# The first 512 tokens of a gated SSM and feed-forward mix: token tiles turned by the matrix engine instead of a transposing DMA, and weight strips taken in order of landing

## The chip, the cores and the metric

The kernel runs on one core of one Trainium2 chip, in one launch. The metric is the device time of the execution in microseconds (us); the time before is the median of nine runs. One execution was also profiled.

Names used below: PE is the matrix engine (TensorE), PEld its weight loads, DVE the vector engine, ACT the scalar engine, POOL GpSimd, SP the sync engine. SP and ACT issue DMAs; their issues are shown as SPq and ACTq.

## The reference

The input `x` has 2048 tokens of 640 channels, in bf16. Three things are computed from it and mixed:

```
g = sigmoid((x * gate_w).sum(-1, keepdims=True))        # one gate for each token
# branch A: diagonal complex state-space layer, P = 640 states
Lam_bar = exp(exp(log_dt) * Lam)
B_bar   = ((Lam_bar - 1) / Lam)[:, None] * (B_re + 1j*B_im)
h_t     = Lam_bar * h_{t-1} + B_bar x_t
a       = 2 * real(h @ C.T) + x * Dskip
# branch B: feed-forward, 640 -> 1728 -> 640
b       = gelu_tanh(x @ w1 + b1) @ w2 + b2
out     = g * a + (1 - g) * b
```

## The kernel before, in words

Tokens are worked in `NCH` = 4 chunks of `CH` = 512, each of four token tiles of `P` = 128. The 640 channels are `KD` = 5 blocks of 128 (`kd` = 0 to 4). A matmul needs the channels on the partitions, so each chunk needs `x` turned: `xT[c]`, of shape 128 x 5 x 512. For chunks 1 to 3 a transposing DMA on SP makes it. For chunk 0 there are two ways side by side. Token tiles 0 and 1 are loaded as they lie (`xn[0]`), and `turn` makes a matmul of the tile against an identity, five per token tile, into a PSUM bank; `turned` copies the bank into `xT[0]`, on DVE or on ACT. Token tiles 2 and 3 (tokens `HT` = 256 to 511) are written by one transposing DMA on SP (line 141).

The first feed-forward matmul (FF1) of chunk 0 fills `FA` = 6 PSUM banks at once, one for each 128-wide block `kf` of the 1728 hidden units. It goes by strips: `strip(kd, t0, t1, first)` issues six matmuls, one for each bank, with the weights `w1a[kd]` (128 x 768) and the tokens `t0` to `t1` (line 247 in `ff1_mm`). So PE can begin a strip as soon as that `w1a[kd]` and that token tile are there. The order before is: kd 0 for tile 0; tile 1 is turned; kd 1 for tile 0; kd 0 and 1 for tile 1; kd 2 for tiles 0 and 1; a small matmul that turns the parameter rows `prmA` (line 322); kd 3 and 4 for tiles 0 and 1; then kd 0 to 4 for tiles 2 and 3 (256 columns each), with a small matmul on `prmB` (line 379) after kd 2. Six gelus on ACT (line 252, with the bias `colB` that comes from `prmB`) empty the six banks. The next hidden blocks use `w1b` and go bank by bank: the first two fill two banks that are free, and the third needs one of the six.

Beside this runs a chain for the rotation tables of the state-space scan: `prmA` is copied to `colA` on DVE (line 323), then one small `Exp` on ACT, small products on DVE, three wide DVE instructions (lines 354 to 356, `u`, `kk`, `red`), the `Sin` activations on ACT (lines 365 to 374), and from line 394 on the DVE work that builds the tables `TCOS` and `TSIN`. The scan of all chunks follows on DVE.

What sets the order. On PE, DVE and ACT the instructions run in the order in which the kernel writes them (`manual_schedule`); an engine's next instruction waits behind the one before it. DMAs run in the order of issue on their queue. The program hands out eight completion semaphores to the DMAs in turn, over both queues, and an issue waits until the earlier DMA with the same semaphore has landed: so the second `w1a` on ACT, `w1a[2]`, is issued when `w1a[0]` has landed, and what is behind it on that queue waits too. The initial issues before are: on SP `xn` tile 0, `xn` tile 1, `w1a[1]`, `w1a[3]`, the transposing DMA, five `w1b`, and then the transposes of the other weights; on ACT `w1a[0]`, three rows of `prmA`, `w1a[2]`, `w1a[4]`, two rows of `prmB`. The program opens with eight matmuls on constants (line 209) that produce nothing.

Activation functions come in tables; the trace shows each change of table on ACT as an `ACT_TABLE_LOAD`.

Of the kernel before, what the change touches and what calls it, by code (L numbers as in the profile page):

```python
# [11 lines left out]
ACT = mybir.ActivationFunctionType  # L12
BF16 = mybir.dt.bfloat16
F32 = mybir.dt.float32
I32 = mybir.dt.int32

P = 128
# [3 lines left out]
CH = 512  # L21
NCH = T // CH
KD = D // P
KS = D // P
KF = (F + P - 1) // P
F_LAST = F - (KF - 1) * P
NT = T // P
TPC = CH // P
H = TPC // 2
HT = H * P  # L30
KSA = 2
HD = D // 2
FA = 6
# [8 lines left out]
def kernel(  # L42
# [19 lines left out]
    nc = tc.nc  # L62
    x2d = A_x.flatten_outer_dims()
# [3 lines left out]
    const = ctx.enter_context(tc.tile_pool(name="const", bufs=1))  # L67
# [7 lines left out]
    def bank(dtype=F32):  # L75
        return ps.tile([P, CH * 4 // (4 if dtype == F32 else 2)], dtype, name="bank")
# [3 lines left out]
    n1b = F - cut1 + 1  # L80
    xT = [const.tile([P, KD, CH], BF16, name=f"xT{c}") for c in range(NCH)]
    w1a = [const.tile([P, cut1], BF16, name=f"w1a_{kd}") for kd in range(KD)]
    w1b = [const.tile([P, n1b], BF16, name=f"w1b_{kd}") for kd in range(KD)]
# [6 lines left out]
    ident = const.tile([P, P], BF16, name="ident")  # L90
    prmA = const.tile([P, P], BF16, name="prmA")
    NB = KS + KF - 1
    prmB = const.tile([P, P], BF16, name="prmB")
    colA = const.tile([P, 3 * KS], F32, name="colA")
    colB = const.tile([P, NB], F32, name="colB")
# [11 lines left out]
    xn = [None] * NCH  # L107
# [4 lines left out]
    b1_c = colB[:, KS:NB]  # L112


    def load_xn(c, a0=0, a1=TPC):
        if a0 == 0:
            xn[c] = xnp.tile([P, TPC, D], BF16, name="xn")
        r0 = c * CH + a0 * P
        nc.sync.dma_start(out=xn[c][:, a0:a1, :], in_=x2d[r0:r0 + (a1 - a0) * P, :].rearrange("(a p) d -> p a d", p=P))

    def load_w1a(queue, kd):
        queue.dma_start(out=w1a[kd][:], in_=B_w1[kd * P:(kd + 1) * P, 0:cut1])  # L122

    def rows(queue, dst, v):
        queue.dma_start(out=dst, in_=v.rearrange("(j p) -> j p", p=P))

    load_xn(0, 0, 1)
    load_w1a(nc.scalar, 0)
    load_xn(0, 1, H)
    nc.vector.memset(prmA[:], 0.0)  # L130
    nc.vector.memset(prmB[:], 0.0)
    rows(nc.scalar, prmA[0:KS, :], A_log_dt)
    rows(nc.scalar, prmA[KS:2 * KS, :], A_Lambda_im)
    rows(nc.scalar, prmA[2 * KS:3 * KS, :], A_Lambda_re)
    load_w1a(nc.sync, 1)
    load_w1a(nc.scalar, 2)
    load_w1a(nc.sync, 3)
    load_w1a(nc.scalar, 4)
    rows(nc.scalar, prmB[KS:NB, :], B_b1[0:(KF - 1) * P])
    rows(nc.scalar, prmB[0:KS, :], gate_w)  # L140
    nc.sync.dma_start_transpose(out=xT[0][:, :, HT:CH], in_=x2d[HT:CH, :])
    for kd in range(KD):
        nc.sync.dma_start(out=w1b[kd][:, 0:F - cut1], in_=B_w1[kd * P:(kd + 1) * P, cut1:F])
    make_identity(nc, ident[:])
# [15 lines left out]
    nc.sync.dma_start(out=Dbc[:], in_=A_Dskip.rearrange("(o d) -> o d", o=1).to_broadcast([P, D]))  # L160
    nc.sync.dma_start_transpose(out=xT[2][:], in_=x2d[2 * CH:3 * CH, :])
    nc.sync.dma_start_transpose(out=xT[3][:], in_=x2d[3 * CH:4 * CH, :])
    load_xn(0, H, TPC)
    load_xn(1)

    ctx.enter_context(tc.manual_schedule(engines={E.PE, E.DVE, E.Activation}))
# [28 lines left out]
    def pe(cols):  # L195
        ck.pe += cols / 2400.0 + 0.002
# [7 lines left out]
    tf = const.tile([P, HC], F32, name="tf")  # L204
    nc.vector.tensor_copy(out=tf[:], in_=tfi[:])
    ones = lambda n: nc.const_aps.tensor(1.0, [P, n], BF16)
    pA = bank()
    for n in (512, 512, 512, 512, 512, 512, 128, 128):
        nc.tensor.matmul(pA[:, 0:n], lhsT=ones(P), rhs=ones(n), start=True, stop=True)

    def turn(p, col, a, kd):
        nc.tensor.matmul(p[:, col:col + P], lhsT=xn[0][:, a, kd * P:(kd + 1) * P], rhs=ident[:], start=True, stop=True,
                         skip_group_check=True)

    def turned(engine, p, col, a, k0, k1):
        dst = xT[0][:, k0:k1, a * P:(a + 1) * P]
        src = p[:, col:col + (k1 - k0) * P].rearrange("p (k t) -> p k t", t=P)
        if engine is nc.vector:
            nc.vector.tensor_copy(out=dst, in_=src)
        else:  # L220
            nc.scalar.activation(out=dst, in_=src, func=ACT.Identity)

    tA, tB = bank(), bank()
# [4 lines left out]
    turned(nc.vector, tB, 0, 0, 1, 3)  # L228
    for i in range(2):
        turn(pA, i * P, 0, 3 + i)  # L230
    turned(nc.vector, pA, 0, 0, 3, 5)

    def col(name, dtype=F32, n=KS):
        return const.tile([P, n], dtype, name=name)
# [7 lines left out]
    hs = [None] * NCH  # L242
    gel = [None] * NCH
    gbs = [None] * NT
    def ff1_mm(p, c, kf, kd, t0=0, t1=CH, first=None):
        w = w1a[kd][:, kf * P:(kf + 1) * P] if kf < FA else w1b[kd][:, (kf - FA) * P:(kf - FA + 1) * P]
        nc.tensor.matmul(p[:, t0:t1], lhsT=w, rhs=xT[c][:, kd, t0:t1],  # L247
                         start=(kd == 0) if first is None else first, stop=(kd == KD - 1), skip_group_check=first is not None)
        pe(t1 - t0)

    def ff1_act(p, c, kf):
# [31 lines left out]
    def ff1(c, k0=0, at={}):  # L283
        for kf in range(k0, KF - 1):
            if kf in at:
                at[kf]()
            p = bank()
            if kf == KF - 3:
                last = last_bank(c)
            for kd in range(KD):  # L290
                ff1_mm(p, c, kf, kd)
            ff1_act(p, c, kf)
            let_out(ck.pe)
        last_tile(c, *last)
        let_out(ck.pe)
# [6 lines left out]
    gel_tile(0)  # L302
    banks = [bank() for _ in range(FA)]

    def strip(kd, t0, t1, first):
        for kf in range(FA):
            ff1_mm(banks[kf], 0, kf, kd, t0, t1, first)

    strip(0, 0, P, True)
    tB = bank()  # L310
    for i in range(4):
        turn(tB, i * P, 1, i)
    turned(nc.vector, tB, 0, 1, 0, 1)
    turned(nc.vector, tB, P, 1, 1, 2)
    turned(nc.scalar, tB, 2 * P, 1, 2, 4)
    turn(pA, 0, 1, 4)
    turned(nc.scalar, pA, 0, 1, 4, 5)
    strip(1, 0, P, False)
    strip(0, P, HT, False)
    strip(1, P, HT, False)  # L320
    strip(2, 0, HT, False)
    nc.tensor.matmul(pA[:, P:P + 3 * KS], lhsT=prmA[:], rhs=ident[:, 0:3 * KS], start=True, stop=True, skip_group_check=True)
    nc.vector.tensor_copy(out=colA[:], in_=pA[:, P:P + 3 * KS])
    nc.scalar.activation(out=dt16[:], in_=ldt_c, func=ACT.Exp)
    nc.vector.tensor_copy(out=dt32[:], in_=dt16[:])
    nc.vector.tensor_tensor(out=dtl[:], in0=dt32[:], in1=lre_c, op=ALU.mult)
# [33 lines left out]
    sQ, cQ = sq[:, 3 * KS:4 * KS], cq[:, 3 * KS:4 * KS]  # L360


    for kd in range(3, KD):
        strip(kd, 0, HT, False)
    nc.scalar.activation(out=FS[:, :, 0:HC], in_=red, func=ACT.Sin, scale=TWO_PI_M)
    nc.vector.scalar_tensor_tensor(out=ab, in0=red, scalar=-1.0, in1=red, op0=ALU.mult, op1=ALU.max)
    nc.scalar.activation(out=FC[:, :, 0:HC], in_=ab, func=ACT.Sin, scale=-TWO_PI_M, bias=halfpi[:])
# [4 lines left out]
    nc.vector.scalar_tensor_tensor(out=absq[:], in0=redq[:], scalar=-1.0, in1=redq[:], op0=ALU.mult, op1=ALU.max)  # L372
    nc.scalar.activation(out=sq[:], in_=redq[:], func=ACT.Sin, scale=TWO_PI_M)
    nc.scalar.activation(out=cq[:], in_=absq[:], func=ACT.Sin, scale=-TWO_PI_M, bias=halfpi[:])
    for kd in range(KD):
        for kf in range(FA):
            ff1_mm(banks[kf], 0, kf, kd, HT, CH)
        if kd == 2:
            nc.tensor.matmul(pA[:, 0:NB], lhsT=prmB[:], rhs=ident[:, 0:NB], start=True, stop=True)  # L379
            nc.vector.tensor_copy(out=colB[:], in_=pA[:, 0:NB])  # L380
            for j in range(KD):
                nc.vector.tensor_copy(out=w1b[j][:, n1b - 1:n1b], in_=pA[:, j:j + 1])
    for kf in range(FA):
        ff1_act(banks[kf], 0, kf)
    two_banks = [bank(), bank()]
# [327 lines left out]
```

## Time and profile before

| | us |
|---|---|
| median of nine runs | 219.26 |
| lowest, highest of the nine | 218.48, 221.66 |
| the profiled execution, its own time | 221.09 |
| its span in the profile | 219.3 |
| PE busy in the span (97%) | 212.0 |
| DVE busy (86%) | 189.4 |
| ACT busy (46%) | 100.5 |

The profile counts from the start of its span; the profiled execution's own time is 1.79 us more than the span, and it is the second longest of the nine. Instructions of one group are merged in a timeline: the start is that of the first, the length reaches to the end of the last. A digit in a row of 40 slices is a share in tenths of a slice of 5.48 us; `PEclk` is the clock that was granted to PE.

### The profile page before, as it was taken

How to read it: one execution, taken by the hardware profiler on the slowest of the kernel's cores; microseconds unless marked ns; L12 is line 12 of the kernel's file. 1: busy time of each engine (PE TensorE's matmuls, PEld its weight loads, DVE VectorE, ACT ScalarE, POOL GpSimd, SP SyncE). 2: the span in 40 equal slices, each digit the busy share in tenths (PEclk: the TensorE clock that was granted, in tenths of full speed). 3: DMA queues.
4: the chain of work that ended last, by engine and by line, in shares of the span. 5: the costliest groups of instructions: out<-in, count | busy, mean ns of one | idle time of the engine just before them, and what ended most of it. 6: DMA issues, size and time to landing. Idle time of an engine off the chain costs nothing.

```text
span 219.3 us, 3534 instructions
## 1 busy us (share of the span) xinstructions
PE 212.0 (97%) x1381; PEld 119.0 (54%) x1381; DVE 189.4 (86%) x396; ACT 100.5 (46%) x180; POOL 1.0 (0%) x8
## 2 busy tenths in 40 slices
PE   8589999999999999999999999999999999999994
PEld 4465544445445544576445477544454567654773
DVE  2459999999999999898999999999999999983152
ACT  0649755666596587601580420255674333204200
POOL 1000000000000000000000000000000000000000
PEclk9969999999999999999999999999999999999999
DMA  6998999998000000024000005200000000100011
GB/s 183 138 251 182 190 233 303 275 202 219 0 3 0 0 3 0 1 54 170 30 0 0 3 0 160 82 0 1 0 1 15 0 3 30 60 30 3 0 63 60
DMA packets 31618, 16.16 MB, mean 74 GB/s; under 512 B 24178, under 2 KB 31602, under 8 KB 31602
## 3 DMA queue, kind: packets, MB, share of 16 engines
q1 hardware_dynamic: 30960, 15.31, 30.4%
q10 hardware_dynamic: 642, 0.63, 1.4%
q8 instruction: 11, 0.18, 0.3%
q14 instruction: 5, 0.04, 0.1%
HBM read 7.48 MB, written 2.62 MB: 46 GB/s over the span
## 4 chain that ended last, share of the span: by engine, by line
PE 93%; DMA 5%; ACTq 0%; DVE 0%; issue 0%
PE bank L580 26%; PE bank L247 25%; PE bank L639 20%; PE bank L522 20%; DMA w1a<-in_B_w_dram 5%; PE bank L596 1%; PE bank L273 1%; ACTq L122 0%; DVE ot L644 0%; PE bank L263 0%; PE bank L379 0%
## 5 line engine op out<-in xcount | busy, mean ns | idle before, releaser
L580 PE MATMUL bank<-w_sb,gel 128*128 128x512 bf16 (+1 forms) x416 | 57.9, 299 | 0.0
L580 PEld LDWEIGHTS <-gel 128*128 128x128 bf16 x416 | 32.3, 98 | 25.5
L525 ACT ACTIVATE bu<-bank 128x512 bf16<-128x512 f32 x40 | 23.9, 597 | 39.4 <-PE bank L522 38.9
L252 ACT ACTIVATE gel<-bank,colB 128x512 bf16<-128x512 f32 x52 | 34.2, 692 | 12.3 <-PE bank L247 11.5
L639 PEld LDWEIGHTS <-hs 128*128 128x128 bf16 x330 | 31.6, 98 | 11.6
L476 DVE TENSOR_TENSOR_SCAN g<-r_c,carry,v 128x512 bf16<-128x512 f32 x30 | 37.4, 1271 | 0.0
L247 PE MATMUL bank<-xT,w1a 128*128 128x512 bf16 (+2 forms) x162 | 29.4, 344 | 3.3 <-DMA w1a<-in_B_w_dram 3.3
L588 ACT ACTIVATE gb<-bank,gcol 128x512 f32<-128x512 f32 (+1 forms) x32 | 15.1, 526 | 35.5 <-PE bank L596 19.4
L247 PE MATMUL bank<-xT,w1b 128*128 128x512 bf16 x140 | 31.0, 379 | 0.0
L639 PE MATMUL bank<-CT_im,hs 128*128 128x320 bf16 (+2 forms) x165 | 27.1, 295 | 0.0
L639 PE MATMUL bank<-CT_re,hs 128*128 128x320 bf16 (+2 forms) x165 | 27.1, 295 | 0.0
L644 DVE SCALAR_TENSOR_TENSOR ot<-bank,gcol,gb 128x320 bf16<-128x320 f32 (+2 forms) x33 | 17.5, 531 | 9.5 <-PE bank L639 8.7
L522 PE MATMUL bank<-xT,BT_re 128*128 128x512 bf16 x100 | 24.8, 379 | 0.0
L522 PE MATMUL bank<-xT,BT_im 128*128 128x512 bf16 x100 | 24.8, 379 | 0.0
L247 PEld LDWEIGHTS <-w1a 128*128 128x128 bf16 x162 | 15.9, 106 | 15.6 <-DMA w1a<-in_B_w_dram 3.9
L247 PEld LDWEIGHTS <-w1b 128*128 128x128 bf16 x140 | 13.7, 98 | 16.2
L555 DVE TENSOR_TENSOR bank<-xn,Dbc 128x320 f32<-128x320 bf16 (+2 forms) x33 | 14.5, 480 | 3.4 <-ACT gb L588 3.3
L522 PEld LDWEIGHTS <-BT_im 128*128 128x128 bf16 x100 | 9.8, 98 | 11.8
L522 PEld LDWEIGHTS <-BT_re 128*128 128x128 bf16 x100 | 9.6, 98 | 11.0
L457 DVE TENSOR_TENSOR v<-wa,wb 128x512 bf16<-128x512 bf16 x40 | 15.2, 420 | 0.5
L569 ACT ACTIVATE bank<-b2bc 128x512 f32<-128x512 bf16 (+1 forms) x24 | 11.7, 529 | 6.3 <-DVE ot L644 6.3
L457 DVE TENSOR_TENSOR wa<-TCOS,g 128x1024 bf16<-128x1024 bf16 x20 | 13.7, 685 | 0.1
(98 smaller groups left out, 147.6 us busy)
## 6 DMA issues: line engine op xcount, KB each, us to landing
out_dram<-ot SPq DMA_DIRECT2D x15, 160.0 KB, 1.8
w_sb<-in_B_w_dram SPq DMA_DIRECT2D x1, 2080.0 KB, 10.3
xn<-in_A_x_dram SPq DMA_DIRECT2D x3, 640.0 KB, 4.8
w1b<-in_B_w_dram SPq DMA_DIRECT2D x5, 240.0 KB, 6.5
w1a<-in_B_w_dram ACTq DMA_DIRECT2D x3, 192.0 KB, 4.1
w1a<-in_B_w_dram SPq DMA_DIRECT2D x2, 192.0 KB, 3.8
xn<-in_A_x_dram SPq DMA_DIRECT2D x2, 160.0 KB, 2.9
xn<-in_A_x_dram SPq DMA_DIRECT2D x1, 320.0 KB, 4.2
```

The lines of the kernel that those rows point to most:

```text
L247: nc.tensor.matmul(p[:, t0:t1], lhsT=w, rhs=xT[c][:, kd, t0:t1], start=(kd == 0) if first is None else first, stop=(kd == KD - 1), skip_gr ...
L252: nc.scalar.activation(out=gel[c][:, kf, :], in_=p[:, :], func=ACT.Gelu_apprx_tanh, bias=b1_c[:, kf:kf + 1])
L457: nc.vector.tensor_tensor(out=o, in0=a, in1=b, op=op)
L476: nc.vector.tensor_tensor_scan(s["g"][:, ri, :], r_c[:, ks:ks + 1].to_broadcast([P, CH]), s["v"][:, ri, :], init, ALU.mult, ALU.add)
L522: nc.tensor.matmul(p[:], lhsT=BT[ks >= KSA][:, kd, (ks % KSA if ks < KSA else ks - KSA) * P:][:, 0:P], rhs=xT[c][:, kd, :], start=(kd == 0 ...
L525: nc.scalar.activation(out=bu[:, ri, :], in_=p[:], func=ACT.Identity)
L555: dve_now(ck.pe, 0.45, lambda: nc.vector.tensor_tensor(out=p[:, 0:d1 - d0], in0=xn[c][:, a, d0:d1], in1=Dbc[:, d0:d1], op=ALU.mult))
L569: nc.scalar.activation(out=v, in_=src, func=ACT.Identity)
L580: nc.tensor.matmul(p[:, col:col + d1 - d0], lhsT=gel[c][:, kf, a * P:(a + 1) * P], rhs=w2_sb[:, kf, d0:d1], start=False, stop=False, skip_ ...
L588: nc.scalar.activation(out=gbs[ti][:, d0:d1], in_=p[:, col:col + d1 - d0], func=ACT.Identity, scale=gcol[:, 1, ti:ti + 1])
L639: nc.tensor.matmul(p[:, 0:d1 - d0], lhsT=hs[c][:, j, lo:lo + P], rhs=CT[:, j % KS, d0:d1], start=False, stop=(j == 2 * KS - 1), skip_group ...
L644: nc.vector.scalar_tensor_tensor(out=ot[:, d0:d1], in0=p[:, 0:d1 - d0], scalar=gcol[:, 0, ti:ti + 1], in1=gbs[ti][:, d0:d1], op0=ALU.mult, ...
```

## The change

Token tiles 2 and 3 are loaded as they lie (`xn[0]`) and turned on PE like tiles 0 and 1; the transposing DMA of chunk 0 and the later load of `xn[0]`'s second half go away. `turn_all(a)` is the helper for tiles 1 to 3: three turns into a bank, two copies on DVE, two turns into `pA`, one copy on ACT.

The issues are dealt anew. SP: `xn` tile 0, tile 1, `w1a[1]`, `w1a[3]`, three `prmA` rows, `xn` tile 3, two `prmB` rows, then `w1b` as before. ACT: `w1a[0]`, `w1a[2]`, `w1a[4]`, `xn` tile 2. The first eight of these take the eight semaphores for the first time; the `prmA` rows then wait for `w1a[0]`, `xn` tile 0 and `xn` tile 1, `xn` tile 3 waits for `w1a[2]`, the `prmB` rows for `w1a[1]` and `w1a[4]`, and the first `w1b` for `w1a[3]`.

The strips are taken in the order kd 0, 2 (tiles 0 and 1 one by one), 1, 4, 3 (both together), the `prmA` matmul standing before kd 3. Tile 2 is turned in the middle of the kd 3 strip; kd 0 and 2 of tile 2 follow, then tile 3 is turned, then kd 1 of tile 2, kd 0, 2, 1 of tile 3, the `prmB` matmul, and kd 3 and 4 of tiles 2 and 3 together. A one-element `Exp` on ACT (`warm`) is put behind ACT's DMA issues.

```diff
-    load_xn(0, 1, H)
+    load_xn(0, 1, 2)
+    load_w1a(nc.scalar, 2)
+    load_w1a(nc.sync, 1)
+    load_w1a(nc.scalar, 4)
+    load_w1a(nc.sync, 3)
+    load_xn(0, 2, 3, nc.scalar)
...
-    rows(nc.scalar, prmA[0:KS, :], A_log_dt)
...
-    load_w1a(nc.sync, 1)
-    load_w1a(nc.scalar, 2)
-    load_w1a(nc.sync, 3)
-    load_w1a(nc.scalar, 4)
...
-    nc.sync.dma_start_transpose(out=xT[0][:, :, HT:CH], in_=x2d[HT:CH, :])
+    rows(nc.sync, prmA[0:KS, :], A_log_dt)
+    rows(nc.sync, prmA[KS:2 * KS, :], A_Lambda_im)
+    rows(nc.sync, prmA[2 * KS:3 * KS, :], A_Lambda_re)
+    load_xn(0, 3, 4)
+    rows(nc.sync, prmB[KS:NB, :], B_b1[0:(KF - 1) * P])
+    rows(nc.sync, prmB[0:KS, :], gate_w)
...
-    load_xn(0, H, TPC)
...
+    nc.scalar.activation(out=warm[:], in_=ones(1), func=ACT.Exp)
...
-    turned(nc.vector, pA, 0, 0, 3, 5)
+    turned(nc.scalar, pA, 0, 0, 3, 5)
...
+    def turn_all(a):
+        tB = bank()
+        for i in range(3):
+            turn(tB, i * P, a, i)
+        turned(nc.vector, tB, 0, a, 0, 1)
+        turned(nc.vector, tB, P, a, 1, 3)
+        for i in range(2):
+            turn(pA, i * P, a, 3 + i)
+        turned(nc.scalar, pA, 0, a, 3, 5)
 
     strip(0, 0, P, True)
...
-    strip(1, 0, P, False)
-    strip(0, P, HT, False)
-    strip(1, P, HT, False)
-    strip(2, 0, HT, False)
+    turn_all(1)
+    strip(2, 0, P, False)
+    strip(0, P, HT, False)
+    strip(2, P, HT, False)
+    strip(1, 0, HT, False)
+    strip(4, 0, HT, False)
...
-    for kd in range(3, KD):
-        strip(kd, 0, HT, False)
+    strip(3, 0, HT, False, 0, 3)
+    turn_all(2)
+    strip(3, 0, HT, False, 3, FA)
+    strip(0, HT, HT + P, True)
+    strip(2, HT, HT + P, False)
+    turn_all(3)
+    strip(1, HT, HT + P, False)
     nc.scalar.activation(out=FS[:, :, 0:HC], in_=red, func=ACT.Sin, scale=TWO_PI_M)
...
-    for kd in range(KD):
-        for kf in range(FA):
-            ff1_mm(banks[kf], 0, kf, kd, HT, CH)
-        if kd == 2:
...
+    for kd in (0, 2, 1):
+        strip(kd, HT + P, CH, kd == 0)
...
+    for kd in (3, 4):
+        strip(kd, HT, CH, False)
```

More of the change, by code (lines that the diff above doesn't have):

```diff
@@ L112, with load_xn @@
     b1_c = colB[:, KS:NB]
-    def load_xn(c, a0=0, a1=TPC):
+    def load_xn(c, a0=0, a1=TPC, queue=None):
         if a0 == 0:
@@ L118, in load_xn @@
         r0 = c * CH + a0 * P
-        nc.sync.dma_start(out=xn[c][:, a0:a1, :], in_=x2d[r0:r0 + (a1 - a0) * P, :].rearrange("(a p) d -> p a d", p=P))
+        (queue or nc.sync).dma_start(out=xn[c][:, a0:a1, :], in_=x2d[r0:r0 + (a1 - a0) * P, :].rearrange("(a p) d -> p a d", p=P))
     def load_w1a(queue, kd):
@@ L128 @@
     load_w1a(nc.scalar, 0)
-    load_xn(0, 1, H)
+    load_xn(0, 1, 2)
[4 more added lines that the diff above has]
+    load_xn(0, 2, 3, nc.scalar)
     nc.vector.memset(prmA[:], 0.0)
     nc.vector.memset(prmB[:], 0.0)
-    rows(nc.scalar, prmA[0:KS, :], A_log_dt)
-    rows(nc.scalar, prmA[KS:2 * KS, :], A_Lambda_im)
-    rows(nc.scalar, prmA[2 * KS:3 * KS, :], A_Lambda_re)
-    load_w1a(nc.sync, 1)
-    load_w1a(nc.scalar, 2)
-    load_w1a(nc.sync, 3)
-    load_w1a(nc.scalar, 4)
-    rows(nc.scalar, prmB[KS:NB, :], B_b1[0:(KF - 1) * P])
-    rows(nc.scalar, prmB[0:KS, :], gate_w)
-    nc.sync.dma_start_transpose(out=xT[0][:, :, HT:CH], in_=x2d[HT:CH, :])
+    rows(nc.sync, prmA[0:KS, :], A_log_dt)
[4 more added lines that the diff above has]
+    rows(nc.sync, prmB[0:KS, :], gate_w)
     for kd in range(KD):
@@ L206 @@
     ones = lambda n: nc.const_aps.tensor(1.0, [P, n], BF16)
+    warm = const.tile([P, 1], F32, name="warm")
+    nc.scalar.activation(out=warm[:], in_=ones(1), func=ACT.Exp)
     pA = bank()
@@ L244, with ff1_mm @@
     gbs = [None] * NT
-    def ff1_mm(p, c, kf, kd, t0=0, t1=CH, first=None):
+    def ff1_mm(p, c, kf, kd, t0=0, t1=CH, first=None, last=KD - 1):
         w = w1a[kd][:, kf * P:(kf + 1) * P] if kf < FA else w1b[kd][:, (kf - FA) * P:(kf - FA + 1) * P]
         nc.tensor.matmul(p[:, t0:t1], lhsT=w, rhs=xT[c][:, kd, t0:t1],
-                         start=(kd == 0) if first is None else first, stop=(kd == KD - 1), skip_group_check=first is not None)
+                         start=(kd == 0) if first is None else first, stop=(kd == last), skip_group_check=first is not None)
         pe(t1 - t0)
@@ L303, with strip @@
     banks = [bank() for _ in range(FA)]
-    def strip(kd, t0, t1, first):
-        for kf in range(FA):
-            ff1_mm(banks[kf], 0, kf, kd, t0, t1, first)
-    strip(0, 0, P, True)
[L310 to L317, printed above, removed]
-    strip(1, 0, P, False)
-    strip(0, P, HT, False)
-    strip(1, P, HT, False)
-    strip(2, 0, HT, False)
-    nc.tensor.matmul(pA[:, P:P + 3 * KS], lhsT=prmA[:], rhs=ident[:, 0:3 * KS], start=True, stop=True, skip_group_check=True)
-    nc.vector.tensor_copy(out=colA[:], in_=pA[:, P:P + 3 * KS])
+    def strip(kd, t0, t1, first, f0=0, f1=FA):
+        for kf in range(f0, f1):
+            ff1_mm(banks[kf], 0, kf, kd, t0, t1, first, 3 if t0 < HT else KD - 1)
+    def turn_all(a):
[7 more added lines that the diff above has]
+        turned(nc.scalar, pA, 0, a, 3, 5)
+    strip(0, 0, P, True)
+    turn_all(1)
+    strip(2, 0, P, False)
+    strip(0, P, HT, False)
+    strip(2, P, HT, False)
+    strip(1, 0, HT, False)
+    strip(4, 0, HT, False)
+    nc.tensor.matmul(pA[:, 0:3 * KS], lhsT=prmA[:], rhs=ident[:, 0:3 * KS], start=True, stop=True, skip_group_check=True)
+    nc.vector.tensor_copy(out=colA[:], in_=pA[:, 0:3 * KS])
     nc.scalar.activation(out=dt16[:], in_=ldt_c, func=ACT.Exp)
@@ L374 @@
     nc.scalar.activation(out=cq[:], in_=absq[:], func=ACT.Sin, scale=-TWO_PI_M, bias=halfpi[:])
-    for kd in range(KD):
-        for kf in range(FA):
-            ff1_mm(banks[kf], 0, kf, kd, HT, CH)
-        if kd == 2:
[L379 to L382, printed above, removed]
+    for kd in (0, 2, 1):
+        strip(kd, HT + P, CH, kd == 0)
+    nc.tensor.matmul(pA[:, 0:NB], lhsT=prmB[:], rhs=ident[:, 0:NB], start=True, stop=True, skip_group_check=True)
+    nc.vector.tensor_copy(out=colB[:], in_=pA[:, 0:NB])
+    for j in range(KD):
+        nc.vector.tensor_copy(out=w1b[j][:, n1b - 1:n1b], in_=pA[:, j:j + 1])
+    for kd in (3, 4):
+        strip(kd, HT, CH, False)
     for kf in range(FA):
```

## The prediction, made before the changed kernel was run

> **What bounds the kernel now.** I read the page first: the granted clock by slices and the shares of the chain that ended last.
>
> ```profile
> PEclk9969999999999999999999999999999999999999
> PE 93%; DMA 5%; ACTq 0%; DVE 0%; issue 0%
> ```
>
> The end is set by PE, which works almost without a break; 5% of the chain is DMA, and in one of the first slices the clock was only 0.6. So I went to the chain in order of time, which says where that 5% lies.
>
> ```profile
> 0.73 3.08 DMA w1a<-in_B_w_dram
> ...
> 4.23 7.51 DMA w1a<-in_B_w_dram
> ...
> 11.79 4.22 PE bank L247 x24
> ...
> 16.03 6.94 PE bank L247 x37
> ```
>
> `w1a[4]`, issued on ACT at 4.23, took 7.51 us to land, while the transposing DMA was under way. From 11.79 on the chain is PE alone, up to the last 0.4 us. Whatever the change does must show before about 20 us. The timeline of PE, with start, length, and in brackets the idle time before:
>
> ```profile
> 5.56 1.44 PE L247 MATMUL bank<-xT,w1a 128*128 128x128 bf16 x18
> ...
> 7.93 0.83 PE L247 MATMUL bank<-xT,w1a 128*128 128x256 bf16 x6 [0.93 <-DMA w1a<-in_B_w_dram]
> 8.59 0.17 PE L322 MATMUL bank<-ident,prmA 128*128 128x15 bf16 x1
> 8.62 0.81 PE L247 MATMUL bank<-xT,w1a 128*128 128x256 bf16 x6
> 11.79 4.22 PE L247 MATMUL bank<-xT,w1a 128*128 128x256 bf16 x24 [2.35 <-DMA w1a<-in_B_w_dram]
> ```
>
> Two waits for weights, 0.93 and 2.35 us: this is what the change is aimed at. The windows of half a microsecond (stretch; its length; busy time of PE, PEld, DVE, ACT, POOL; granted clock; DMA share; GB/s) show what follows the second:
>
> ```profile
> 12.50:13.00 0.50, 0.50 (x7) 0.45 (x5) 0.50 (x2) 0.44 (x1) 0.00 (x0) 0.96 1.05 365
> 13.00:13.50 0.50, 0.50 (x5) 0.34 (x3) 0.47 (x6) 0.43 (x1) 0.00 (x0) 0.50 1.16 338
> ...
> 16.00:16.50 0.50, 0.50 (x6) 0.38 (x3) 0.41 (x6) 0.16 (x1) 0.00 (x0) 0.63 4.26 163
> ```
>
> Some 1.2 us after the pause the clock falls to half until about 16.4. The 36 matmuls of 256 columns and `prmB` between 11.79 and 17.41 would take 36 x 0.11 + 0.06 = 4.02 us at the pace of 7.93 to 8.59 (0.66 us for six, 0.11 each); they took 5.62. The half clock costs 1.6 us. Last, the timelines of DVE and ACT, for the chain of the tables:
>
> ```profile
> 8.83 0.17 DVE L323 COPY colA<-bank 128x15 f32<-128x15 f32 x1 [2.75 <-PE bank L322]
> ...
> 11.35 0.83 DVE L356 TENSOR_TENSOR gel<-gel,bu 128x640 f32<-128x640 f32 x1
> ```
> ```profile
> 9.90 1.28 ACT L365 ACT_TABLE_LOAD   x1
> 12.21 0.74 ACT L365 ACTIVATE hs<-gel 128x640 f32<-128x640 f32 x1 [1.02 <-DVE gel L356]
> 13.06 0.83 ACT L367 ACTIVATE hs<-gel,halfpi 128x640 f32<-128x640 f32 x1
> ...
> 16.34 1.28 ACT L252 ACT_TABLE_LOAD   x1 [2.03 <-DVE colB L380]
> ```
>
> From the `prmA` matmul (8.59) to the end of `red` (11.35 + 0.83 = 12.18) DVE is taken up for 3.59 us. The table for `Sin` is loaded while ACT would wait anyway. Both covers matter below.
>
> **The base of the sum.** The mark M is the start of the third `w1b` bank on PE: 17.41 + 10 x 0.216 = 19.57 (0.216 from 25 matmuls in 5.40 us, 17.41 to 22.81). The profiled execution took 221.09, so T = 201.52 + M, if the rest stays dense. It is 1.83 above the median of 219.26; without the half clock it would be 221.09 - 1.6 = 219.5. So the median execution looks like one in which the clock was kept, and the sum is made for both.
>
> **Change 1: loads.** The transposing DMA goes, and eight loads of 1.47 MB in all go out at once on two queues. The windows of 2 us moved 305 GB/s at 2 to 4 us and 242 at 4 to 6. From 2.0 us this is 1.47 MB by 6.8 or by 8.1; `w1a[1]` and `w1a[4]` (1.11 MB) by 5.6 or 6.6. PE's needs: after the 18 matmuls of 128 columns it is free at 6.83; kd 1 and kd 4 take 0.66 each, so it needs `w1a[4]` at 7.49 and `w1a[3]`, `xn` tile 2 at 8.26 or later. Both waits for weights are gone. The Trainium skill, page "DMA: Bandwidth & Descriptors", section "Issuing engines are not separate DMA queues", speaks against the second queue: it only saves time of issuing. The two windows beside it show more flow with both queues loaded, though the mixture of transfers differs too; by the page the later pair of figures would hold, and the loads would still be in time.
>
> **Change 2: `prmA` is reached earlier, S = 8.15** (6.83 + 0.66 + 0.66), against 8.59. Its rows now go by SP behind `w1a[3]`; the third waits for `xn` tile 1. Cost bounded: that issue can't end much before 4.4; the quickest nearest row is a token tile, 2.9 us from issue to landing, so 7.3; the slowest undisturbed is 4.1 us for `w1a`, and an issue at 5.4 gives 9.5. I take 8.15, since the row for `b1x`, equally small, took 3.4 us in traffic (5.0 + 3.4 = 8.4). Queued behind this wait on PE are strip kd 3 and all of tiles 2 and 3. The rows moved onto SP also delay `w1b`, but without the transposing DMA (SP was held 4.1 us by it) these start no later than before, and are not needed until 16.
>
> **Change 3: a new wait on DVE.** Tile 2's copies stand behind `u`, `kk` and `red` on DVE. PE has only 0.1 (`prmA`), 0.66 (kd 3) and five turns to do meanwhile. A 128-column pair costs 0.056 (between 0.03 for 65 columns, 20 in 0.61 us, and 0.11 for 256): turns 0.28. It runs dry at 9.2. `red` ends at 8.15 + 3.59 = 11.74, the first copy (0.29 for 128x128, with 0.03 before and 0.05 after) lets PE go on at 12.11: a wait of 2.9 us in the place of 2.35, again long enough to lose the clock. The page "TensorE: Matmul & The Clock Gate" of the skill, section "HAM oscillation — how this bites in real kernels", allows gaps of up to about 3.4 us. The pause of 2.35 us in this trace contradicts that when read as a single gap; by the page neither version would lose the clock and the sum below would end at 220.6; by the row both may, and it ends at 220.6 or 221.3.
>
> **Change 4: work after the wait.** Before: 36 matmuls of 256. After: 36 of 128 (2.02 us), 12 of 256 (1.32), five turns (0.28), `prmB` (0.06). Kd 0 to 12.45; kd 2 has to wait for the second copy (0.42, some of it overlapped), 12.50 to 12.84; turns to 13.12; kd 1 to 13.46; then two short waits for tile 3's copies, kd 0, 2, 1 to 14.63; `prmB` and kd 3, 4 to 16.0; two `w1b` banks to 18.17. At half clock from 12.98 some 1.6 are added: 19.76.
>
> **Change 5: ACT.** It must copy tile 3's last two blocks before the `Sin` table is loaded. Turns visible at 13.32 (0.2 after 13.12); copy 0.38; table 1.28, now with nothing to hide it; `Sin` row to last `Sin` 2.10 (12.21 to 14.31); table for gelu 1.28; first gelu 0.69; 0.05: 13.32 + 0.38 + 1.28 + 2.10 + 1.28 + 0.69 + 0.05 + 0.02 = 19.12. This is M when the clock is kept, 0.95 later than PE alone. DVE's tables start at about 17.1, against 16.51. It costs nothing while DVE's lead lasts: the last `hs` of chunk 0 was written at 90.07, and PE wants its part at about 91.98, 1.9 us of cover. If that were gone, each further 1 us would cost 1 us.
>
> **The sum.** Clock kept: T = 201.52 + 19.12 = 220.6. Half clock: 201.52 + 19.76 = 221.3. The added turns and smaller matmuls are worth little; the gain of the two waits (3.3 us) is eaten by a new wait of 2.9, and in executions that kept their clock before, ACT's chain adds another 1. I forecast 220.9.
>
> **Rivals.** *Slower still, rows late:* `prmA` at 9.5 shifts the whole chain by 1.35: M = 20.5, T = 222.0. For it: five small rows behind 0.72 MB on one queue. Against: they are issued by 5.0. *Earlier, about the same:* S = 7.3, if the clock is up sooner and the rows land quickly; all is 0.85 earlier, M = 18.27, T = 219.8. For it: PE's 128-column matmuls before 6.1 ran at about 0.1 each, and needn't. Against: the rows. *Faster:* DVE and ACT don't hold PE, the clock stays up: PE goes on from 9.2 through 3.68 us of work and 2.16 of `w1b`, M = 15.04, T = 216.6. It decides from `red` ending before 9; anything faster than 218.16 asks for M below 16.6. Against it stands the order on DVE, with 3.59 us of measured work before the copy. That the waits for weights don't go away at all is the late case again.
>
> **How the numbers follow.** Forecast (220.2 to 221.8) 0.54, late 0.13, earlier 0.20, faster 0.13. One measurement of this kernel can tell about 0.5% from no change: 218.16 and 220.36 bound "same". Of the forecast 0.09 falls below 220.36, so same is 0.29, slower 0.45 + 0.13 = 0.58, faster 0.13. The range 218.9 to 222.2 takes in the early and late bounds and leaves out the faster case and a little of the late one.
>
> **What would show it.** Right: no wait of PE for `w1a` after 5.6; `prmA` at 7.3 to 9.5; a wait of 2 to 3 us before a 128-column strip, put down to DVE's `xT`; `ACT_TABLE_LOAD` for `Sin` after 13; first gelu later than 17.64; perhaps a wait before a `w1b` bank on ACT. Wrong: DVE's copy of tile 2 within 1 us of its turns; a third `w1b` bank before 16.6; any wait of PE at 90 to 92 for `hs`, which would mean that DVE's cover was too small.

## The result, and the profile after

The changed kernel took 221.69 us (median; 220.69 to 222.21), against 219.6 for the kernel before in the same comparison: a ratio of 1.0094, 95% interval 1.0075 to 1.0114. It is 0.9% slower, on the side that had 0.58, 0.8 us above the predicted 220.9 and inside the range. The profiled execution took 221.92 us with a span of 220.1 (before: 221.09 and 219.3). The page of the changed kernel, granted clock and shares of the chain that ended last:

```profile
PEclk9969999999999999999999999999999999999999
PE 95%; DVE 2%; DMA 1%; issue 0%; ACT 0%; DVEq 0%
```

The DMA on the chain fell from 5% to 1%, DVE rose from nothing to 2%, and the clock still dips in the third slice. PE's timeline over the first 21 us (start, length, idle time before it in brackets):

```profile
5.63 2.93 PE L249 MATMUL bank<-xT,w1a 128*128 128x128 bf16 x30
8.51 0.17 PE L328 MATMUL bank<-ident,prmA 128*128 128x15 bf16 x1
...
9.14 0.49 PE L249 MATMUL bank<-xT,w1a 128*128 128x256 bf16 x3
12.39 0.86 PE L249 MATMUL bank<-xT,w1a 128*128 128x128 bf16 x12 [2.76 <-DVE xT L221]
...
17.63 3.62 PE L249 MATMUL bank<-xT,w1b 128*128 128x512 bf16 x16
```

Neither of the waits for `w1a` (0.93 and 2.35 us before) is left: PE works from 5.63 to 9.63 with no break above 0.15 us. Then it stands for 2.76 us, and the releaser is DVE's copy of token tile 2. The reason lies on DVE; on ACT the `Sin` table comes late. From the timelines of DVE and of ACT:

```profile
8.79 0.17 DVE L329 COPY colA<-bank 128x15 f32<-128x15 f32 x1 [2.50 <-PE bank L328]
...
11.31 0.82 DVE L362 TENSOR_TENSOR gel<-gel,bu 128x640 f32<-128x640 f32 x1
12.05 0.62 DVE L221 CAST xT<-bank 128x128 bf16<-128x128 f32 x2
```
```profile
13.81 0.38 ACT L223 ACTIVATE xT<-bank 128x256 bf16<-128x256 f32 x1 [3.69 <-PE bank L214]
14.22 1.28 ACT L376 ACT_TABLE_LOAD   x1
...
18.59 3.00 ACT L254 ACTIVATE gel<-bank,colB 128x512 bf16<-128x512 f32 x5
```

Tile 2 was turned by 9.3, but its two copies on DVE wait behind `u`, `kk` and `red`, until 12.05. The `Sin` table, hidden before at 9.90, is loaded at 14.22, and the first gelu starts at 18.59. The windows of half a microsecond (columns as in the prediction):

```profile
12.50:13.00 0.50, 0.50 (x12) 0.50 (x10) 0.17 (x1) 0.00 (x0) 0.00 (x0) 1.00 0.95 310
13.00:13.50 0.50, 0.50 (x9) 0.50 (x7) 0.00 (x0) 0.00 (x0) 0.00 (x0) 0.56 0.65 153
...
16.00:16.50 0.50, 0.50 (x7) 0.44 (x5) 0.09 (x1) 0.50 (x2) 0.00 (x0) 0.53 0.04 3
```

The clock falls to half just after 13.0 and comes back just before 16.5, as it did before (12.96 to 16.37 there). The chain in order of time (start, length):

```profile
12.13 0.21 DVE xT L221
...
12.39 0.86 PE bank L249 x12
...
16.36 6.83 PE bank L249 x37
```

Where before a DMA of 7.51 us stood ahead of PE's work, it is now DVE's chain. The mark M, the start of the third `w1b` bank, is 17.63 + 10 x 0.216 = 19.79, against 19.57: in these two profiles, both with a half clock, the first 20 us came out 0.22 us longer.

### The profile page after: what moved, and what is told of

Its sections match the earlier page's. It is cut to its first block, busy times and chain, and to the rows that moved or that the text cites. A ratio compares the mean times of both kernels' runs of the same rounds, so it can differ in the third digit from the quotient of the medians.

```text
span 220.1 us, 3597 instructions
## 1 busy us (share of the span) xinstructions
PE 212.6 (97%) x1409; PEld 120.6 (55%) x1409; DVE 190.4 (86%) x399; ACT 101.1 (46%) x183; POOL 1.0 (0%) x8
## 4 chain that ended last, share of the span: by engine, by line
PE 95%; DVE 2%; DMA 1%; issue 0%; ACT 0%; DVEq 0%
PE bank L249 26%; PE bank L591 26%; PE bank L650 20%; PE bank L533 20%; DMA xn<-in_A_x_dram 1%; PE bank L607 1%; PE bank L275 1%; PE bank L214 1%; DVE gel L360 0%; DVE gel L362 0%; DVE bu L361 0%; DVE ot L655 0%; ACT dt L330 0%; DVE xT L221 0%; DVE colA L329 0%
## 5 line engine op out<-in xcount | busy, mean ns | idle before, releaser
L249 PEld LDWEIGHTS <-w1a 128*128 128x128 bf16 x180 | 17.0, 108 | 13.9 <-issue 2.9
```

## The experiments

Each time has its own comparison with the kernel before, since the times of that kernel differ between comparisons by some tenths of a microsecond; ratios with 95% intervals. "Kept" (the clock stayed up) are executions with a mean granted clock of 0.995 or more; the profile of a version shows one execution of it alone.

**DVE's copies first.** `u`, `kk` and `red` moved behind the copies of tiles 2 and 3.

```diff
-    nc.vector.tensor_tensor(out=u, in0=tf[:].rearrange("p (o i) -> p o i", o=1).to_broadcast([P, KS, HC]), in1=over(thp_c[:]), op=ALU.mult)
-    nc.vector.tensor_copy(out=kk[:], in_=u)
-    nc.vector.tensor_tensor(out=red, in0=u, in1=kk[:], op=ALU.subtract)
...
     strip(1, HT, HT + P, False)
+    nc.vector.tensor_tensor(out=u, in0=tf[:].rearrange("p (o i) -> p o i", o=1).to_broadcast([P, KS, HC]), in1=over(thp_c[:]), op=ALU.mult)
+    nc.vector.tensor_copy(out=kk[:], in_=u)
+    nc.vector.tensor_tensor(out=red, in0=u, in1=kk[:], op=ALU.subtract)
     nc.scalar.activation(out=FS[:, :, 0:HC], in_=red, func=ACT.Sin, scale=TWO_PI_M)
```

> The changed kernel with u, kk and red written behind the copies of tiles 2 and 3 on DVE; nothing else. Theory A (PE waits for DVE's order of work): PE's wait of 2.76 us before the first strip of tile 2 shrinks to 0.5 to 1.0, the six banks are complete about 2 us sooner, but red, and with it the Sin activations and the first gelu, end no sooner than before (first gelu 18.3 to 18.6), so that PE now waits some 2 us before the third w1b bank and the time is 220 to 222: the wait moves from DVE to ACT. Theory B (the data of tile 2 or the rows of prmA are late): the wait stays at about 2.8 us and the time does not change.

Measured: 220.24 us, ratio 1.0075 (1.0034 to 1.0115). From its timeline of PE:

```profile
10.26 0.83 PE L249 MATMUL bank<-xT,w1a 128*128 128x128 bf16 x12 [0.51 <-DVE xT L221]
...
16.30 4.92 PE L249 MATMUL bank<-xT,w1b 128*128 128x512 bf16 x22 [1.95 <-DVE w1b L391]
```

The wait of 2.76 us fell to 0.51, so the order on DVE was its cause. But 1.95 us came back later. The releaser there is DVE again, by another path than ACT's gelus: the second of the two `w1b` banks takes the PSUM of `pA`, which DVE must first read into `colB` and `w1b`, and that now stands behind the delayed products. M is 16.30 + 9 x 0.216 = 18.24. Expected was ACT as the cause, with a first gelu at 18.3 to 18.6; it came at 17.49, and by its end at 18.18 it would have freed the third bank's PSUM at about the same time as DVE did, so the two chains are equally late here.

**The copies of tiles 2 and 3 on ACT**, and `r_c` after them.

```diff
-        turned(nc.vector, tB, 0, a, 0, 1)
-        turned(nc.vector, tB, P, a, 1, 3)
+        if a == 1:
+            turned(nc.vector, tB, 0, a, 0, 1)
+            turned(nc.vector, tB, P, a, 1, 3)
+        else:
+            turned(nc.scalar, tB, 0, a, 0, 3)
...
-    nc.scalar.activation(out=r_c[:], in_=dtl[:], func=ACT.Exp)
...
     strip(1, HT, HT + P, False)
+    nc.scalar.activation(out=r_c[:], in_=dtl[:], func=ACT.Exp)
```

> The changed kernel with all copies of tiles 2 and 3 on ACT (and r_c computed after them), so that DVE goes straight on to u, kk and red. Theory A: wait before the first strip of tile 2 about 0.5 us; Sin from about 13.4 and first gelu at about 16.8 instead of 18.6; third w1b bank at 17.3 to 17.8 instead of 19.8; time 219.3 to 220.3 where the clock is kept, that is about the kernel before. Theory B: no change. Theory C (it is the clock alone that costs): the time falls only in executions whose clock is not lost.

Measured: 218.68 us, ratio 0.9981 (0.9953 to 1.0009), the clock kept in all 12 executions; that is 0.6 us better than the expected range. From the timelines of its PE and ACT:

```profile
9.26 1.46 PE L249 MATMUL bank<-xT,w1a 128*128 128x256 bf16 x15
...
11.81 1.28 ACT L379 ACT_TABLE_LOAD   x1
...
16.18 5.31 ACT L254 ACTIVATE gel<-bank,colB 128x512 bf16<-128x512 f32 x9
```

Tile 2's strip (12 of these 15 matmuls) starts at 9.89, after a wait of 0.3 us, the table is loaded 2.4 us earlier, and the first gelu starts 2.4 us earlier. The loss is gone (1.0094 to 0.9981, about 2.5 us). Nothing was changed in the loads, the turns or the strips. Part of it is the clock, which the changed kernel mostly loses: against the executions of the kernel before that kept it too (218.53 in the same comparison) this version is 0.15 us slower.

**The pause filled, in both kernels.** Matmuls on constants before tile 2's strip in the changed kernel (18 of 256 columns), and before strip kd 4 in the kernel before (20).

```diff
     strip(3, 0, HT, False, 3, FA)
+    for _ in range(18):
+        nc.tensor.matmul(pA[:, 256:512], lhsT=ones(P), rhs=ones(256), start=True, stop=True, skip_group_check=True)
     strip(0, HT, HT + P, True)
```

> The changed kernel with 18 matmuls of 256 columns on constants put on PE where it waits for the copy of tile 2; they compute nothing that is used. Theory A: the clock is kept in nearly all executions (mean granted clock 1.0 instead of 0.992), PE goes on at the same 12.4, ACT's chain then sets the third w1b bank at about 19.2 with a wait of PE of about 0.9, and the time is 220.7 to 221.2, 0.6 to 0.9 less than the changed kernel. Theory C (the clock alone costs): the time falls by 1.6 to 2, to that of the kernel before.

> The kernel before with 20 matmuls of 256 columns on constants put on PE where it waits for w1a[4]; they compute nothing that is used. If the half clock explains the two groups of times of the kernel before, then all executions keep the clock (1.0) and lie at 218.3 to 219.6, and those of the kernel before that run beside it with a mean clock of 0.992 lie 1.5 to 2 us above those with 1.0. If the clock does not matter, the times stay spread from 218 to 222.

Measured: the changed kernel 220.86 us, ratio 1.0075 (1.004 to 1.011); the kernel before 219.36 us, ratio 1.0027 (0.9996 to 1.0057). Both kept the clock in all executions. From the changed kernel's PE and ACT:

```profile
10.23 2.18 PE L373 MATMUL bank<-const-bfloat16-1.0 128*128 128x256 bf16 x18 [0.54 <-ACT xT L223]
...
13.99 1.28 ACT L378 ACT_TABLE_LOAD   x1
...
19.11 2.10 PE L249 MATMUL bank<-xT,w1b 128*128 128x512 bf16 x9 [0.62 <-ACT gel L254]
```

With the clock kept, the third `w1b` bank waits for ACT's first gelu and M is 19.11. So the clock is worth only 19.79 - 19.11 = 0.7 us in the changed kernel: ACT's chain stands right behind it. In the kernel before, M is 15.81 + 10 x 0.216 = 17.97 in this way. There the filler costs something itself: 219.36 is 0.8 us above the executions without it that kept the clock in the same comparison (218.53, 24 of 33), and 1.7 us below those at half clock (221.07, 9 of 33; the two groups lie 2.5 us apart, where 1.5 to 2 was expected).

**The rows early.** `prmA`'s rows through GpSimd's queue, and the `prmA` matmul with its chain three strips earlier (strips kd 2 of tile 1, kd 1 and kd 4 behind it).

```diff
-    rows(nc.sync, prmA[0:KS, :], A_log_dt)
...
+    rows(nc.gpsimd, prmA[0:KS, :], A_log_dt)
...
     strip(0, P, HT, False)
-    strip(2, P, HT, False)
-    strip(1, 0, HT, False)
-    strip(4, 0, HT, False)
     nc.tensor.matmul(pA[:, 0:3 * KS], lhsT=prmA[:], rhs=ident[:, 0:3 * KS], start=True, stop=True, skip_group_check=True)
...
     nc.vector.tensor_tensor(out=red, in0=u, in1=kk[:], op=ALU.subtract)
+    strip(2, P, HT, False)
+    strip(1, 0, HT, False)
+    strip(4, 0, HT, False)
```

> The changed kernel with the three prmA rows loaded by GpSimd's queue at the start, and the prmA matmul with the chain behind it (colA to red) written three strips earlier, before kd 2 of tile 1. The copies stay on DVE behind red. Theory A (PE waits because the copies stand behind u, kk and red): red ends at 9.3 to 10.2 instead of 12.1, PE's wait before the first strip of tile 2 falls from 2.8 to under 0.8, the first gelu comes at 16.3 to 17.0 and the third w1b bank at 17.0 to 17.8: time 218.8 to 220.0. Theory B (the data of tile 2 are late): the wait stays.

Measured: 219.83 us, ratio 1.0011 (0.998 to 1.0042). From its PE:

```profile
7.78 0.17 PE L325 MATMUL bank<-ident,prmA 128*128 128x15 bf16 x1 [1.47 <-DMA prmA<-in_A_Lambda_re_dram]
...
11.59 0.83 PE L249 MATMUL bank<-xT,w1a 128*128 128x128 bf16 x12 [1.05 <-DVE xT L221]
```

The wait fell from 2.76 to 1.05 us, but a new one of 1.47 for the rows appeared, because by this queue they took 4.9 to 5.2 us to land, until about 7.7. So `red` ended at 11.33 and not at 9.3 to 10.2, the first gelu started at 17.51, and M is 18.25: all later than expected, only the time is inside its range.

**Rows early, tile 2's copies on ACT, the `Sin` table fetched early:** the run before, and with it `turn_all(2)` copying on ACT alone, a one-element `Sin` after `r_c`, and the two wide `Sin` ahead of tile 3's turn.

```diff
+        if a == 2:
+            turned(nc.scalar, tB, 0, a, 0, 1)
+            turned(nc.scalar, tB, P, a, 1, 3)
...
     nc.scalar.activation(out=r_c[:], in_=dtl[:], func=ACT.Exp)
+    nc.scalar.activation(out=warm[:], in_=ones(1), func=ACT.Sin)
...
-    strip(2, HT, HT + P, False)
-    turn_all(3)
-    strip(1, HT, HT + P, False)
     nc.scalar.activation(out=FS[:, :, 0:HC], in_=red, func=ACT.Sin, scale=TWO_PI_M)
...
+    strip(2, HT, HT + P, False)
+    turn_all(3)
+    strip(1, HT, HT + P, False)
```

> As the one with early rows, and besides: tile 2 copied on ACT, the Sin table loaded right after r_c (by a one-element Sin), and the two wide Sin activations written before tile 3 is turned. Theory A: neither DVE nor ACT holds PE any more; first gelu at 14.5 to 15.3, third w1b bank set by PE alone at about 16.0 to 16.6 without a wait; clock kept in all; time 217.4 to 218.6, below both kernels' medians. If something else sets the start (loads), the time stays near 218.7.

Measured: 218.69 us, ratio 0.9964 (0.9933 to 0.9995). The waits for copies are 0.24 and 0.23 us, the first gelu starts at 15.48, and no wait is left before the `w1b` banks. But PE waits 1.75 us for the rows, until 7.95, M is 17.12 where 16.0 to 16.6 was expected, and 3 of the 12 executions ran with a half clock (219.56 to 219.81; the 9 kept ones have a median of 218.49).

**The loads alone.** The change's queues, its `warm` activation and its strips of tiles 0 and 1 stay, but tiles 2 and 3 come by the transposing DMA on SP, behind the `prmA` rows, and are worked 256 columns at a time.

```diff
-    load_xn(0, 2, 3, nc.scalar)
...
-    load_xn(0, 3, 4)
+    nc.sync.dma_start_transpose(out=xT[0][:, :, HT:CH], in_=x2d[HT:CH, :])
...
-    strip(3, 0, HT, False, 0, 3)
-    turn_all(2)
-    strip(3, 0, HT, False, 3, FA)
-    strip(0, HT, HT + P, True)
-    strip(2, HT, HT + P, False)
-    turn_all(3)
-    strip(1, HT, HT + P, False)
+    strip(3, 0, HT, False)
...
-        strip(kd, HT + P, CH, kd == 0)
+        strip(kd, HT, CH, kd == 0)
```

> One part alone: queues, order of landing and strips of tiles 0 and 1 as in the changed kernel, but tiles 2 and 3 turned by the transposing DMA, issued on SP behind the prmA rows in the place of the load of tile 3, and taken in 256-column strips. Theory A (the loss is the wait for the copies, not the loads): no wait for w1a; PE waits for the transposing DMA until 10.5 to 13 and ACT's Sin table is loaded while it waits, so that the first gelu is not late; third w1b bank 16.6 to 18.5; time 218 to 220, not slower than the kernel before by more than 0.3%. Rival (the new order of loads costs by itself): over 220.5 with kept clocks.

Measured: 217.67 us, ratio 0.9918 (0.9888 to 0.9947), the clock kept in all executions. From its PE and ACT:

```profile
7.87 0.17 PE L328 MATMUL bank<-ident,prmA 128*128 128x15 bf16 x1
7.90 2.79 PE L249 MATMUL bank<-xT,w1a 128*128 128x256 bf16 x24
...
9.23 1.28 ACT L370 ACT_TABLE_LOAD   x1
...
13.77 5.35 PE L249 MATMUL bank<-xT,w1b 128*128 128x512 bf16 x24 [1.53 <-DVE w1b L385]
```

No wait for a weight or for the transposing DMA is left (one until 10.5 to 13 was expected, and a time of 218 to 220), and the table is hidden again. So what is left of the change here, new queues and strips in order of landing, is a gain of 0.8%, and turning tiles 2 and 3 on PE, as the change orders it, costs 1.0094 - 0.9918, about 1.8% or 3.9 us, the lost clock included. What is late next is DVE's read of `pA` (1.53 us). In the table of DMA issues (last figure: us from issue to landing), first of the kernel before, then of this one:

```profile
xT<-in_A_x_dram SPq DMA_TRANSPOSE x1, 8.7
```
```profile
xT<-in_A_x_dram SPq DMA_TRANSPOSE x1, 4.0
```

**And the rows first.** The same with `prmA`'s rows ahead of `w1a[1]` and `w1a[3]` on SP, its matmul and chain ahead of kd 4, and kd 4 ahead of kd 1.

```diff
-    load_w1a(nc.sync, 1)
-    load_w1a(nc.scalar, 4)
-    load_w1a(nc.sync, 3)
...
     rows(nc.sync, prmA[2 * KS:3 * KS, :], A_Lambda_re)
+    load_w1a(nc.scalar, 4)
+    load_w1a(nc.sync, 1)
+    load_w1a(nc.sync, 3)
```

> The version with the new loads and the transposing DMA, and besides the prmA rows issued on SP ahead of w1a[1] and w1a[3], the prmA matmul with its chain before kd 4, and kd 4 before kd 1. If the tables' chain (prmA to Sin to gelu) is what holds PE at the w1b banks there, as in the changed kernel with a kept clock, then prmA comes at 6.0 to 6.6 instead of 7.87, the first gelu at 13.2 to 13.8 instead of 14.95, PE's wait of 1.53 before the second w1b bank falls under 0.8, and the time is 216.0 to 217.0. If the later issue of w1a[1] and w1a[3] (they now wait for xn tile 0 and w1a[0]) costs as much on PE, the time stays at 217.5 to 218.5.

Measured: 216.72 us, ratio 0.9864 (0.9831 to 0.9896), faster than both kernels. From its PE:

```profile
6.15 0.17 PE L326 MATMUL bank<-ident,prmA 128*128 128x15 bf16 x1
...
14.47 3.84 PE L249 MATMUL bank<-xT,w1b 128*128 128x512 bf16 x17 [0.66 <-DMA w1b<-in_B_w_dram]
```

`prmA` comes 1.7 us earlier, DVE's read of `pA` no longer holds PE, and the `w1b` loads are the next limit; the transposing DMA holds PE for 0.33 us at 8.30.

**Only the order of issue, in the kernel before:** its four later `w1a` issued ahead of the parameter rows.

```diff
     load_xn(0, 1, H)
+    load_w1a(nc.scalar, 2)
+    load_w1a(nc.sync, 1)
+    load_w1a(nc.scalar, 4)
+    load_w1a(nc.sync, 3)
...
-    load_w1a(nc.sync, 1)
-    load_w1a(nc.scalar, 2)
-    load_w1a(nc.sync, 3)
-    load_w1a(nc.scalar, 4)
```

> The kernel before with one thing changed: the four later w1a are issued before the prmA and prmB rows, so that w1a[2] and w1a[4] are behind nothing on ACT's queue and wait for no semaphore. Strips, turns and the transposing DMA stay. If the two waits for w1a came from the late issue on ACT behind the rows and not from the order of strips, w1a[4] lands at 6 to 8 instead of 11.74, PE's wait of 2.35 is gone, the clock is kept, and the time is 217.3 to 218.5. If the transposing DMA itself holds the weights back, w1a[4] still lands after 9.5 and the time stays at 219 to 220.

Measured: 219.47 us, ratio 0.9997 (0.9967 to 1.0026): the expected gain did not come. The profiled execution, at 218.25 the fastest of the 12, kept its clock; 5 of the 12 did not. In it the weights landed within 4.5 us of their issue and the wait of 2.35 us went, but another stood in its place on PE:

```profile
8.26 0.81 PE L247 MATMUL bank<-xT,w1a 128*128 128x256 bf16 x6 [1.07 <-ACT xT L221]
```

ACT was held in its issues of `prmB`'s rows until 6.45 and copied tile 1 only after its table load, at 7.83. So issuing the weights first is not enough by itself. In the version with the loads alone the rows are off ACT's queue, `warm` has fetched the table by 3.42, before the copy needs it, and the strips stand in another order; no run tells these three apart.

**The two kernels once more**, unaltered, for the end of the span.

> The changed kernel once more, unaltered, beside the kernel before. Question: in the profiles so far the time from the third w1b bank on PE (the mark M) to the end is 198.6 to 198.8 us plus the time from the last DVE write of ot to the end of the span, which was 2.9 us before, 3.4 after, 3.5, 3.3 and 3.2 in the runs that keep all queues of the change, and 2.7 to 3.0 in the others. Theory A: the long tail belongs to these queues; then this profile shows 3.2 to 3.5 again and the executions with a kept clock have a median near 221.0. Theory B: it scatters from execution to execution; then it can as well be 2.7 to 3.0, and the time 0.5 lower. In both, M at 19.1 (clock kept) or 19.8 (half clock), a wait of 2.6 to 2.9 us before tile 2's strip for DVE's copy, and a ratio of 1.007 to 1.011.

> The kernel before once more, for one profile: theory A expects 2.7 to 3.0 us from the last write of ot to the end of the span, theory B anything from 2.7 to 3.5. M at 17.0 to 18.2 if the clock is kept, 19 to 19.8 if it falls to half, so 218.6 to 219.8 or 220.5 to 221.5 us.

Measured: the changed kernel 221.54 us, ratio 1.011 (1.0065 to 1.0155); the kernel before 218.51 us in its one execution. PE's wait of each, the changed kernel first:

```profile
12.21 0.83 PE L249 MATMUL bank<-xT,w1a 128*128 128x128 bf16 x12 [2.76 <-DVE xT L221]
```
```profile
10.46 2.81 PE L247 MATMUL bank<-xT,w1a 128*128 128x256 bf16 x24 [1.28 <-DMA w1a<-in_B_w_dram]
```

The wait for DVE is 2.76 us again: from the `prmA` matmul to this wait neither PE nor DVE waits for a load, in either profile. The wait for `w1a[4]` is 1.28, not 2.35 (`w1a[4]` took 6.2 us to land, not 7.5), and this execution kept its clock: the landing of that load varies from one execution to another. Its time of 218.51 is just under the expected 218.6 to 219.8.

All profiles together, from M, the end of the last DVE write of `ot` and the span (us):

| kernel | M | last write - M | span - last write | own time |
|---|---|---|---|---|
| before | 19.57 | 196.87 | 2.9 | 221.09 |
| after | 19.79 | 196.87 | 3.5 | 221.92 |
| copies first | 18.24 | 196.89 | 3.4 | 220.35 |
| copies on ACT | 16.92 | 196.86 | 3.3 | 218.91 |
| after, filled | 19.11 | 196.86 | 3.3 | 221.03 |
| before, filled | 17.97 | 196.93 | 2.9 | 219.60 |
| rows early | 18.25 | 196.87 | 2.7 | 219.61 |
| rows and `Sin` early | 17.12 | 196.87 | 2.7 | 218.49 |
| loads alone | 15.71 | 196.88 | 3.0 | 217.36 |
| rows first | 14.90 | 196.89 | 3.0 | 216.68 |
| issue order only | 16.70 | 196.88 | 2.9 | 218.25 |
| after again | 19.62 | 196.87 | 3.3 | 221.53 |
| before again | 16.88 | 196.88 | 2.9 | 218.51 |

M is read as the start of PE's last stretch without a wait in the first two `w1b` banks, plus 0.216 us for each of their ten matmuls in it, or, where that is later, the first gelu's end plus 0.05. From M to the last write every kernel takes the same 196.9 us. All differences are made before M, or behind the last write. (In the repeat of the kernel before one of the ten matmuls has no record, and PE pauses for 0.28 us before the ninth, which starts at 16.45.)

## Why the prediction was right

**The base of the sum** held: T follows M one for one. Only the stretch behind the last write, taken over as 2.9 us, is not the same: it is 3.3 to 3.5 in the five profiles that keep all queues of the change, and 2.7 to 3.0 in all others. The repeat (3.3 again) speaks for a property of these kernels and against scatter. It is 0.4 to 0.6 us of the missing 0.8, a term that the sum didn't have. The traces show what happens there: in these five an 8 KB packet of an instruction queue (q14 in the profile's list of DMA queues) starts 1.0 to 1.1 us after the last write, among the packets of ACT's last output, which end at 1.56 to 1.74 us; in the eight others that packet starts at 2.4 us or later, and the output's packets end at 1.17 to 1.20. Why the packet comes early in just these kernels stays open; no run was made on that.

**Change 1, loads.** Right for the changed kernel, with less room than predicted: PE pauses 0.15 us before kd 1 in one profile and not at all in the repeat, but waits for `w1a[1]` 0.27 us in the run with the copies first and 0.83 in the one with the copies on ACT, which have the same loads. In the latter `w1a[1]` let PE go on at 7.31, against a predicted landing of 5.6 to 6.6. The run with the loads alone shows what the new queues and strips were worth: 0.8%. That `w1b` would start no later than before was wrong (first issue 7.89 against 5.67), but in the changed kernel PE never waited for it.

**Change 2, `prmA`.** Predicted 8.15, bounds 7.3 to 9.5; measured 8.51 and, once more, 8.32. The late and the early rival fell with that (9.5 and 7.3).

**Change 3, the wait on DVE.** Predicted 2.9 us, with PE going on at 12.11; measured 2.76 and 12.39, the difference being the later `prmA`. The run with the copies first shows that DVE's order was the cause of the wait; the runs with the copies on ACT show that with this wait and the late `Sin` table gone the loss is gone as well.

**Change 4, PE's work and the clock.** M at half clock: predicted 19.76, measured 19.79 and 19.62. That it fits to 0.03 is luck: PE went on 0.28 us later than predicted (12.39), and its work from there to the `w1b` banks took 5.24 us instead of the predicted 5.50. The weighing was off: both cases were taken as about equal, but with the half clock 21 of 25 executions of the changed kernel ran, and 25 of 85 of the kernel before beside the experiments. The skill's page "TensorE: Matmul & The Clock Gate" (section "HAM oscillation — how this bites in real kernels") allows gaps of up to about 3.4 us; read for a single gap, the pauses of 2.76 us contradict it, as that of 2.35 did.

**Change 5, ACT's chain.** M with the clock kept: predicted 19.12, and 19.11 measured with the pause filled. The path is the predicted one, the second digit is luck: ACT's copy started 0.28 us late, at 13.60, and the `Sin` row took 1.76 us instead of 2.10. It needed its own run, since the half clock hides it. DVE's cover of 1.9 us held: PE shows no wait for `hs` at 90.

**The sum.** 196.87 + 3.3 + 1.79 (execution outside its span) + M gives 221.1 with the clock kept and 221.8 at half; measured medians are 221.0 (four executions) and 221.7. The predicted 220.6 and 221.3 lack the 0.4 to 0.6 of the end. The rest of the 0.8 is the weighing. On the side of before, the one profile stood for more than it could: it was an execution with a late `w1a[4]`. A kept execution was put at 219.5; the medians of kept ones were 218.5 to 219.3. So the ratio of 1.0094 mixes two cases: with the clock kept in both kernels the changed one is 1.7 to 2.5 us slower (221.0), and at half clock in both by at most 0.7 (221.7 against 221.0 to 221.5 in the four comparisons; in the last of them, side by side, 221.55 and 221.53).

**The rival "faster"** asked for DVE and ACT not to hold PE. The run with the copies on ACT took PE's long wait away; it reached M = 16.92, not 15.04, since the gelus still come after ACT's `Sin`. The loads alone and the rows first reach M = 15.71 and 14.90, so a start that early is possible, but both keep the transposing DMA; no run reached it with tiles 2 and 3 turned on PE.

## What to carry to other kernels

When a transfer is replaced by work on engines, follow the copies that belong to it: the turns on PE cost little, but their copies stood behind 3.59 us of other work on DVE, and the wait they made (2.76 us) was about as long as the two removed (0.93 and 2.35). A load that is late may only be issued late or held up by what else is in flight: with the transposing DMA kept, new queues and strips in order of landing gave 0.8%, where replacing it as well lost 0.9%. Issuing the weights first alone gave nothing, since another wait took the place of the one removed. Where the clock or another wait hides a chain, take the cover away in a run of its own, because it is what limits next.

## What the runs showed of the hardware

- The transposing DMA of 256 tokens landed 7.5 to 8.7 us after its issue in the kernel before (8.7 also with the pause filled), and 3.9 to 4.2 us after it in the three kernels that issue all `w1a` ahead of it. With nothing but the order of issue changed it was 4.2, so its length depends on what was in flight beside it.
- A pause of PE of 2.35 or 2.76 us was followed, 0.7 to 1.2 us after its end, by 3.41 us of half clock; pauses of 1.28, 1.53 and 1.95 us in other profiles were not. The length of the pause alone does not decide it: 4 of 25 executions of the changed kernel kept the clock, and 13 of 48 lost it in four versions whose profiled pauses were all under 2 us (copies first, both with the rows early, issue order only).
- In all 13 profiles the granted clock changed only at whole multiples of 3.41 us after it first rose (before: 6.13, 12.96, 16.37; after: 6.23, 13.06, 16.47). Cut into such steps, the step just ahead of the half clock had PE idle for 2.24 of its 3.41 us before, and for 2.74 and 2.19 in the two profiles of the changed kernel. Over the 13 profiles, the end of the span included, every step with 2.12 us or more of idle time was followed by a half clock, and none with 1.91 or less. This fits the mixed outcomes: a pause of 2.76 us can be shared by two steps, and short pauses can add up in one. No run moved a pause on purpose to test it.
- Rows of 1.2 KB by GpSimd's queue took 4.9 to 5.2 us to land and were waited for until 7.8 and 7.95 us, hardly earlier than on SP behind two weights, where `prmA` was turned at 7.87 without a wait.
- The time behind the last write was 2.7 to 3.0 or 3.3 to 3.5 us, although the last output DMAs are the same; in the long cases an instruction packet ran among the last output's packets, which then ended about 0.4 to 0.6 us later.
